# A second unit's inverses, masks and last weight piece moved in the written order of a fused attention and expert kernel

## The chip, the cores and the metric

The kernel runs on one core of a Trainium2 chip. Its engines work side by side and wait for each other on semaphores: TensorE (PE, with its weight loads shown apart as PEld), VectorE (DVE), ScalarE (ACT), GpSimd (POOL) and SyncE (SP), which here only issues transfers. ACT can issue transfers too. The metric is the time of one execution on the device in microseconds. Four runs of the kernel before gave a median of 562.54 us (561.25 to 563.91).

## The reference

The first half is a gated linear recurrence over 4 batches, 8 heads, 768 tokens and a head width of 48; the second is an expert layer with an ELU between two products, over 3072 tokens, 384 columns and 2048 hidden columns.

```python
f = 1.0 / (1.0 + np.exp(-f_logit))
for t in range(S):
    state = f[:, :, t, :, None] * state + np.einsum('bhd,bhe->bhde', k[:, :, t], v[:, :, t])
    y[:, :, t] = np.einsum('bhd,bhde->bhe', q[:, :, t], state)
...
h = x @ w_in
g = np.where(h > 0.0, h, alpha * (np.exp(np.minimum(h, 0.0)) - 1.0))
return (g @ w_out).astype(np.float32)
```

The attention inputs are float32. The two weight matrices arrive as float64, and the kernel makes float32 of them itself.

## The kernel before

The 3072 tokens are cut into 12 units of 256. A unit's attention is worked in closed form: `gates` makes 1 + exp(-f_logit) on ACT, `grow` (L630) its running product along the tokens on DVE, `fall` (L635) the inverse of that product, and `scale` (L625, POOL) multiplies k by the product and q by the inverse. Three pairs of heads lie in rows of their own and the fourth, pair `NKT`, is spread over the 16-row gaps beside them; `move` (L642) carries the product (`which` 0) or the inverse (`which` 1) of that fourth pair from the gaps into its own rows, in two transfers of 48 KB inside the on-chip memory. For unit 1 the inverse is moved on ACT's queue. Then `advance` (L736) makes the sums that update the states, `scores` (L713) the products of q and k, `mask` (L721) keeps the causal ones, `step` (L694, L699) adds up the states, and `outputs` (L751) and `carried` (L771) make the unit's tokens. `advance` and `outputs` write the same two PSUM banks, so `outputs` waits for the last `step` that reads them.

The weights come in 16 pieces n of 768 KB, one of `w_in` or `w_out` at a time, in the order in which unit 0 needs them. `fetch(n)` loads a piece into one of seven slots of `area`: a w_out piece in one transfer (L548), a w_in piece in a large one (L550, 576 KB) and two for the gaps (L553, 96 KB each). `split(n)` takes two DVE instructions (L567, L571), `lower(n)` one of ACT (L577), and `merge(n)` one of DVE (L585), which writes the float32 weights and then calls `fetch(n + 7)`. So each piece goes DVE, ACT, DVE.

Every transfer reports on one of eight semaphores, which are taken in turn by transfers of SP and ACT alike. A transfer that takes a semaphore again first waits, on the queue that issues it, for the landing of the transfer that had it before.

Everything is written out by hand and each engine runs its instructions in the written order. Work ahead of the loop does unit 0's attention and unit 1's gates. Then comes a loop over steps T (L1176). Two steps make one pair P = T // 2, which is 256 hidden columns of one unit; unit 0 has T = 0 to 15, unit 1 starts at T = 16. An even step does, in this order: `elu(P - 1)` on DVE (L955), whatever `plan` holds for the step, and `up` (for unit 0 L946: 12 matmuls, then Relu and Exp on ACT, L933 and L934). An odd step does the plan and then `down(P - 2)` (for unit 0 L978). At the end of each step the pieces in `later` are split and lowered. From unit 1 on, `up7` (L901) and the lower half of `down` (L1003) use seven products in the place of eight. Their PSUM tiles `psH` are two buffers in rotation, so the second half of `up7(8)` writes where pair 7 of unit 0 was, and waits for `elu(7)` to have read it.

What stands where around the change, before: pieces 2 to 15 are merged at the step of their number and split and lowered two steps earlier; pieces 10 and 11 are lowered at step 10. Unit 1's inverse is moved at step 3 (`F1`), its q of pair `NKT` scaled at step 5, and `both(1)` (advance, scores, masks, states) is planned for step 8 (`A1[1]`), which is before `up(4)`. Piece 15 is split and lowered at step 13, `gates(2)` is planned for step 14 and so lies ahead of `up(7)` and its Relu and Exp. `combine` starts at step 16, and so does unit 2's `grow`.

Of the kernel before, what the change touches and what calls it, by code (L numbers as in the profile page):

```python
# [356 lines left out]
def fast(ctx: ExitStack, tc: tile.TileContext, q, k, v, f_logit, w_in, w_out, out, flag, outer):  # L357
# [18 lines left out]
    nc = tc.nc  # L376
# [7 lines left out]
    NC = U // C  # L384
# [3 lines left out]
    NFT = DFF // 128  # L388
    NKT = DM // 128
# [4 lines left out]
    LAG = 2  # L394
    AHEAD = 7
    WA = 1
    F1 = 3
    W0 = 3
    SMALL = 16
    MORE = 5  # L400
# [2 lines left out]
    A1 = (2, 8, 10, 11)  # L403
# [207 lines left out]
    def gates(u, pieces=(NKT,), bias=1):  # L611

        p = 0
        for n in pieces:
            a = qkf[u % NB]["f"][:, p : p + n, 0]
            nc.scalar.activation(a, a, AF.Exp, scale=-1.0)
            if bias:
                nc.scalar.activation(a, a, AF.Copy, bias=1.0)
            p += n

    def scale(u, *todo):

        t = qkf[u % NB]
        for n, p, e in todo:
            e.tensor_tensor(out=t[n][:, p], in0=t[n][:, p], in1=t["f"][:, p, "kq".index(n)], op=ALU.mult)  # L625
# [6 lines left out]
    def fall(u, p):  # L632

        f = qkf[u % NB]["f"]
        nc.vector.reciprocal(f[:, p, 1], f[:, p, 0])  # L635

    def move(u, which, queue):

        f = qkf[u % NB]["f"]
        for r in range(2):  # L640
            to = PAD + D * r
            queue.dma_start(out=f[to : to + D, NKT, which], in_=f[GAP[r] : GAP[r] + PAD, 0:NKT, which])  # L642

    def decays(u, p):
        grow(u, p)
        fall(u, p)
        scale(u, ("k", p, nc.gpsimd))
        if p:
            scale(u, ("q", p - 1, nc.gpsimd))
        if p == NKT - 1:  # L650
            move(u, slice(0, 2), nc.sync if u > 1 else nc.scalar)

    def watch(u):
        nc.vector.scalar_tensor_tensor(
            out=fine[:], in0=qkf[u % NB]["f"][:, 0:NKT, 0, U - 1 :], scalar=LIMIT, in1=fine[:],
            op0=ALU.is_le, op1=ALU.mult,
        )

    def settle(u):

        watch(u)
        scale(u, ("q", NKT - 1, nc.gpsimd), ("k", NKT, nc.gpsimd), ("q", NKT, nc.gpsimd))
# [22 lines left out]
    def step(u, c):  # L685

        if u % UPB == UPB - 1 and c == NC - 1:
            return
        new = pus[u][c % 2][:, c // 2]
        box = boxes[(u * NC + c) % len(boxes)]  # L690
        s = box[:].rearrange("n (p d) -> n p d", d=64)[:, 0:HP, PAD:]
        if u % UPB or c:
            old = sts[u, c][:].rearrange("n (p d) -> n p d", d=64)[:, 0:HP, PAD:]
            nc.vector.tensor_tensor(out=s, in0=new, in1=old, op=ALU.add)  # L694
        else:
            nc.scalar.copy(s, new)
        if c == NC - 1:
            end = qkf[u % NB]["f"][:, :, 1, U - 1 :].broadcast_to([128, HP, D])
            nc.vector.tensor_tensor(out=s, in0=s, in1=end, op=ALU.mult)  # L699
        sts[(u, c + 1) if c < NC - 1 else (u + 1, 0)] = box  # L700

    def scores(u, banks=("a0", "a1"), pairs=range(HP), pc=None):

        t = qkf[u % NB]
        if pc is None:
            ats[u] = sb.tile([128, 2, NW, HP, C], FP32, tag="at", name=f"at{u}", bufs=1)
            pc = [ps.tile([128, NW, HP, C], FP32, tag=banks[r], name=f"psS{u}_{r}") for r in range(2)]
        for p in pairs:
            for w in range(NW):
                for b in range(2):  # L710
                    cols = slice(w * W + b * C, w * W + b * C + C)
                    for r in range(2):
                        nc.tensor.matmul(  # L713
                            pc[r][FULL[b], w, p], lhsT=t["k"][FULL[r], p, cols], rhs=t["q"][FULL[r], p, cols],
                            start=True, stop=True,
                        )
        return pc

    def mask(u, pc):
        for r in range(2):  # L720
            nc.vector.tensor_tensor(  # L721
                out=ats[u][:, r].rearrange("k w p i -> k (w p) i"), in0=pc[r][:].rearrange("k w p i -> k (w p) i"),
                in1=twice[:].unsqueeze(1).broadcast_to([128, NW * HP, C]), op=ALU.mult,
            )

    def advance(u, pairs=range(HP)):

        if u not in pus:
            pus[u] = [ps.tile([128, NW, HP, D], FP32, tag=n, name=f"psU{u}_{n}") for n in ("a0", "a1")]
        pu = pus[u]  # L730
        for p in pairs:
            for w in range(NW):
                for r in range(2):
                    h = 2 * p + r
                    for b in range(2):
                        nc.tensor.matmul(  # L736
                            pu[b][FULL[r], w, p], lhsT=kn[FULL[b], p, w, FULL[r]],
                            rhs=vs[u % NB][FULL[b], w, PAD + h * D : PAD + (h + 1) * D],
                            start=(w == 0 and p == 0), stop=(w == NW - 1 and p == HP - 1), skip_group_check=True,
                        )  # L740

    def outputs(u, banks=("a0", "a1")):


        pys[u] = [ps.tile([128, NW, HP, C], FP32, tag=banks[b], name=f"psY{u}_{b}") for b in range(2)]
        at = ats.pop(u)
        for w in range(NW):
            for p in range(HP):
                for r in range(2):
                    for b in range(2):  # L750
                        nc.tensor.matmul(  # L751
                            pys[u][b][FULL[r ^ b], w, p], lhsT=of_head(u, b, w, r, p),
                            rhs=at[FULL[b], r, w, p], start=(w == 0 and p == 0), stop=False,
                            skip_group_check=True,
                        )

        for b in range(2):
            nc.scalar.copy(between[:], pys[u][b][:, :, :, 0])
# [71 lines left out]
    plan, later = {}, {}  # L830

    def at_step(step, *todo):
        plan.setdefault(step, []).extend(todo)

    def both(u):

        advance(u)
        mask(u, scores(u, ("m3", "m0")))
        for c in range(NC):
            step(u, c)  # L840

    def attention(u, first, then):

        kept = []
        for p, i in enumerate(first):
            at_step(i, (lambda: settle(u)) if p == NKT else lambda p=p: decays(u, p))
        if u > 1:
            at_step(then[0], lambda: transposed(u, 0, "a0"), lambda: transposed(u, 1, "a1"))
        if len(then) == 4:
            at_step(then[1], lambda: both(u))  # L850
        else:
            at_step(then[1], lambda: advance(u))
            at_step(then[2], *(lambda c=c: step(u, c) for c in range(NC)))
            at_step(then[3], lambda: kept.append(scores(u)), lambda: mask(u, kept[0]))
        if u > 1:
            at_step(then[-2], lambda: outputs(u))
        at_step(then[-1], lambda: carried(u))
# [277 lines left out]
    scale(1, ("k", 0, nc.gpsimd), ("q", 0, nc.gpsimd), ("k", 1, nc.gpsimd), ("k", 2, nc.gpsimd))  # L1135
    scale(1, ("k", NKT, nc.gpsimd))
    fall(1, 2)
    watch(0)
    watch(1)
    scale(1, ("q", 1, nc.gpsimd), ("q", 2, nc.gpsimd))  # L1140
    at_step(A1[2], lambda: outputs(1), lambda: lower(A1[2]), lambda: lower(A1[2] + 1))
    for n in range(1, NFT):
        t = min(max(needs[n][0] - 2, 0), n)
        at_step(t, lambda n=n: merge(n))
        if n > 1:
            later.setdefault(max(t - 2, 0), []).append(n)
    at_step(F1, lambda: move(1, 1, nc.scalar))
    at_step(F1 + 2, lambda: scale(1, ("q", NKT, nc.gpsimd)))
    at_step(A1[0], lambda: transposed(1, 0, "a0"), lambda: transposed(1, 1, "a1"))
    at_step(4, lambda: warm(0, "m3", SMALL))  # L1150
    at_step(22, lambda: warm(0, "a0", MORE))
    attention(1, (), A1)
    at_step(8, lambda: load(2))
    at_step(14, lambda: gates(2))
    attention(2, D2, A2)
    weights = combine()
    for n in range(NFT):
# [5 lines left out]
    for u in range(3, NU):  # L1163
        t = (u - 1) * NFT
# [5 lines left out]
    for n in range(NR):  # L1170
        t = 3 * NFT + (NU - 4) * NFT * n // NR + RR
# [4 lines left out]
    for T in range(NU * NFT):  # L1176
        P = T // 2
        sevens = order[P][0] >= DIRECT
        if T % 2 and sevens:
            joined(P)  # L1180
        if T % 2 == 0 and P and order[P - 1][0] < DIRECT:
            elu(P - 1)
        for f in plan.pop(T, ()):
            f()
        if T % 2 == 0:
            up(P)
        elif P >= LAG and T not in joint:
            if T - 2 in joint:
                down(P - LAG - 1)
            down(P - LAG)  # L1190
        for n in later.pop(T, ()):
            split(n)
            if n not in (A1[2], A1[2] + 1):
                lower(n)
# [53 lines left out]
```

## Time and profile before

| | |
|---|---|
| median of four runs | 562.54 us (561.25 to 563.91) |
| profiled execution | 561.57 us |
| its span, first to last instruction | 559.7 us |
| mean granted TensorE clock | 0.996 |
| PE busy | 543.3 us (97%) |
| DVE busy | 407.0 us (73%) |
| ACT busy | 227.8 us (41%) |
| POOL busy | 292.3 us (52%) |

The page gives shares of the whole span, and the change works in its first 77 us alone. Views that show order are therefore of more use than sums: the chain of work that ended last, in order of time; the timeline of one engine in a window; and the waits, which name who released whom. Times inside the profile count from its first instruction. In a timeline each row has a start, a duration, the engine (SPq and ACTq for transfers that are issued), the line, the tiles written and read, the number of instructions merged into the row, and in brackets the idle time before it with what ended it. A merged row's duration reaches from its first start to its last end, waits included.

### The profile page before, as it was taken

To read this page: it belongs to the slowest core of one execution; us is meant where nothing else is said; L and a number is where in the kernel's file an instruction comes from. 1 tells how busy PE (TensorE), PEld (TensorE's weight loads), DVE (VectorE), ACT (ScalarE), POOL (GpSimd) and SP (SyncE) were. 2 spreads that over 40 slices of the span, in tenths; PEclk is the share of its full clock that TensorE was granted. 3 is DMA by queue.
4 is the path that set the end of the run, shared out by engine and by line. 5 is a ranking of instruction groups with operands and counts; after the bars stand their busy time and mean duration, and the time that the engine had idled before them with its cause. 6 is when DMAs were issued, how large, how long until landed. Compare 5 with 4: busy or idle time off the path is not lost.

```text
span 559.7 us, 15627 instructions
## 1 busy us (share of the span) xinstructions
PE 543.3 (97%) x6358; PEld 508.0 (91%) x6358; DVE 407.0 (73%) x804; ACT 227.8 (41%) x442; POOL 292.3 (52%) x567
## 2 busy tenths in 40 slices
PE   6899989999999999999999999999999999999996
PEld 3477768999999999999999999999999999999995
DVE  8988989786676786785785785786687777735553
ACT  3287853434343333434434343343333343333331
POOL 6600898475374375365466367357257348325332
PEclk9999989999999999999999999999999999999999
DMA  8998971024025226216207207207207302201101
GB/s 205 246 268 241 269 178 43 3 59 113 2 57 146 57 50 170 65 27 181 81 13 193 81 9 191 85 9 191 87 8 188 90 9 71 87 5 33 31 2 35
DMA packets 39474, 54.30 MB, mean 97 GB/s; under 512 B 4032, under 2 KB 29216, under 8 KB 39392
## 3 DMA queue, kind: packets, MB, share of 16 engines
q1 hardware_dynamic: 38592, 52.61, 36.0%
q8 instruction: 52, 0.85, 0.7%
q10 hardware_dynamic: 800, 0.59, 0.5%
q14 instruction: 30, 0.25, 0.2%
HBM read 45.02 MB, written 4.72 MB: 89 GB/s over the span
## 4 chain that ended last, share of the span: by engine, by line
PE 85%; DMA 7%; DVE 3%; ACT 3%; issue 1%; POOL 1%; ACTq 0%; SPq 0%; DVEq 0%; POOLq 0%
PE psH L901 39%; PE psM L1003 36%; DMA area<-in_moe_w_in_dram 4%; PE psY L771 2%; PE psY L751 2%; PE psU_a L736 2%; PE psS L713 2%; ACT area L577 2%; PE psT L673 1%; PE psM L978 1%; DMA f<-f 1%; DMA k<-in_k_dram 1%; DMA area<-in_moe_w_out_dram 1%; DVE bits L567 1%; DVE wi L585 1%
## 5 line engine op out<-in xcount | busy, mean ns | idle before, releaser
L901 PE MATMUL psH<-xt,wi 128*128 128x128 f32 (+1 forms) x1056 | 195.8, 295 | 0.0
L965 POOL TENSOR_TENSOR sums<-gg 128x128 f32<-128x128 f32 x176 | 77.4, 461 | 210.1 <-DVE gg L955 186.9
L933 ACT ACTIVATE gg<-hh 128x512 f32<-128x512 f32 x88 | 55.5, 630 | 252.0 <-DVE hh L923 111.3
L901 PEld LDWEIGHTS psH<-xt,wi 128*128 128x128 f32 x1056 | 150.0, 192 | 1.6
L901 PE MATMUL psH<-xt,area 128*128 128x128 f32 x704 | 121.9, 275 | 2.0 <-DVE gg L955 2.0
L901 PEld LDWEIGHTS psH<-xt,area 128*128 128x128 f32 x704 | 106.8, 192 | 6.8 <-DVE gg L955 2.2
L910 DVE TENSOR_TENSOR hh<-psH,u 128x256 f32<-128x256 f32 x88 | 37.0, 420 | 99.6 <-ACT u L908 99.6
L1003 PE MATMUL psM<-area,sums 128*128 128x192 f32 x528 | 102.1, 326 | 0.1
L1003 PEld LDWEIGHTS psM<-area,sums 128*128 128x128 f32 x528 | 88.0, 190 | 0.2 <-issue 0.2
L1003 PE MATMUL psM<-wo,gg 128*128 128x192 f32 x352 | 73.9, 332 | 0.0
L955 DVE SCALAR_TENSOR_TENSOR gg<-gg,hh 128x512 f32<-128x512 f32 x88 | 63.1, 717 | 1.5 <-ACT gg L934 1.5
L635 DVE RECIPROCAL f<-f 128x256 f32<-128x256 f32 x36 | 62.8, 1748 | 1.1
L934 ACT ACTIVATE gg<-gg 128x512 f32<-128x512 f32 x96 | 60.5, 631 | 3.0
L1003 PEld LDWEIGHTS psM<-wo,gg 128*128 128x128 f32 x352 | 56.3, 190 | 1.4
L923 DVE TENSOR_TENSOR hh<-psH,u43h 128x256 f32<-128x256 f32 (+1 forms) x176 | 54.7, 352 | 3.0
L965 POOL TENSOR_TENSOR sums<-gg,sums 128x128 f32<-128x128 f32 x88 | 46.7, 531 | 6.9
L625 POOL TENSOR_TENSOR q<-q,f 128x256 f32<-128x256 f32 x48 | 39.7, 828 | 18.5 <-DMA area<-in_moe_w_in_dram 14.7
L923 DVE TENSOR_TENSOR u43h<-psH,hh 128x256 f32<-128x256 f32 x88 | 37.1, 421 | 9.4 <-PE psH L901 9.0
L625 POOL TENSOR_TENSOR k<-k,f 128x256 f32<-128x256 f32 x48 | 39.2, 819 | 7.8 <-DMA f<-f 5.5
L965 POOL TENSOR_TENSOR sums<-sums,gg 128x128 f32<-128x128 f32 x88 | 43.3, 492 | 0.0
L1003 PE MATMUL psM<-area,gg 128*128 128x192 f32 x176 | 43.0, 326 | 0.0
L1003 PE MATMUL psM<-wo,sums 128*128 128x192 f32 x176 | 43.0, 326 | 0.0
(100 smaller groups left out, 649.2 us busy)
## 6 DMA issues: line engine op xcount, KB each, us to landing
area<-in_moe_w_out_dram SPq DMA_DIRECT2D x8, 768.0 KB, 10.4
again<-in_moe_w_in_dram SPq DMA_DIRECT2D x16, 384.0 KB, 4.3
again<-in_moe_w_out_dram SPq DMA_DIRECT2D x16, 384.0 KB, 3.6
k<-in_k_dram SPq DMA_DIRECT2D x12, 384.0 KB, 4.5
q<-in_q_dram SPq DMA_DIRECT2D x12, 384.0 KB, 5.6
v<-in_v_dram SPq DMA_DIRECT2D x12, 384.0 KB, 6.1
area<-in_moe_w_in_dram SPq DMA_DIRECT2D x8, 576.0 KB, 8.9
out_dram<-o SPq DMA_DIRECT2D x42, 96.0 KB, 2.6
```

Source lines behind the costliest of these rows:

```text
L577: nc.scalar.activation(raw.bitcast(U16)[:, 2::4], raw.bitcast(U32)[:, 0::2], AF.Copy, scale=2.0**-29)
L625: e.tensor_tensor(out=t[n][:, p], in0=t[n][:, p], in1=t["f"][:, p, "kq".index(n)], op=ALU.mult)
L635: nc.vector.reciprocal(f[:, p, 1], f[:, p, 0])
L713: nc.tensor.matmul(pc[r][FULL[b], w, p], lhsT=t["k"][FULL[r], p, cols], rhs=t["q"][FULL[r], p, cols], start=True, stop=True,)
L901: nc.tensor.matmul(to, lhsT=lhs, rhs=rhs, start=(n == 0), stop=True, skip_group_check=True)
L910: add = lambda to, x, y: nc.vector.tensor_tensor(out=to, in0=x, in1=y, op=ALU.add)
L923: add = lambda to, x, y: nc.vector.tensor_tensor(out=to, in0=x, in1=y, op=ALU.add)
L933: nc.scalar.activation(g[:], h, AF.Relu, scale=-1.0)
L934: nc.scalar.activation(g[:], g[:], AF.Exp, scale=-1.0)
L955: nc.vector.scalar_tensor_tensor(out=g[:], in0=g[:], scalar=-1.0, in1=phs.pop(P), op0=ALU.add, op1=ALU.max)
L965: nc.gpsimd.tensor_tensor(out=s[:, i], in0=x, in1=y, op=op)
L1003: nc.tensor.matmul(pm[bank][:, half * DH : (half + 1) * DH], lhsT=x, rhs=y, start=first, stop=(j == NP - 1), skip_group_check=True,)
```

## The change

Five things move in the written order; no instruction is added or taken away on any engine.

- `move(1, 1, nc.scalar)` goes from step 3 to just behind unit 1's last reciprocal, `fall(1, 2)`, ahead of the loop. It stays on ACT's queue.
- The scaling of unit 1's q of pair `NKT` on POOL, which needs that move, goes from step 5 to ahead of the loop.
- `both(1)` is cut in two: advance, scores and masks go to the end of step 7, ahead of the split of piece 9, and the four states stay at step 8.
- Piece 15 is split and lowered at the end of step 14 in the place of step 13, so behind `up(7)` and its Relu and Exp.
- `gates(2)` goes from step 14 to step 15, behind the lowering of piece 15.

In the built program the two moved transfers also take two other semaphores, two turns of the eight earlier than before, and the transfers of SP between the old and the new place shift by two.

```diff
-    def both(u):
-
-        advance(u)
-        mask(u, scores(u, ("m3", "m0")))
-        for c in range(NC):
+    def both(u, part=3):
+
+        if part & 1:
+            advance(u)
+            mask(u, scores(u, ("m3", "m0")))
+        for c in range(NC if part & 2 else 0):
             step(u, c)
...
-            at_step(then[1], lambda: both(u))
+            at_step(then[1], lambda: both(u, 3 if u > 1 else 2))
...
     fall(1, 2)
+    move(1, 1, nc.scalar)
     watch(0)
     watch(1)
-    scale(1, ("q", 1, nc.gpsimd), ("q", 2, nc.gpsimd))
+    scale(1, ("q", 1, nc.gpsimd), ("q", 2, nc.gpsimd), ("q", NKT, nc.gpsimd))
...
         if n > 1:
-            later.setdefault(max(t - 2, 0), []).append(n)
-    at_step(F1, lambda: move(1, 1, nc.scalar))
-    at_step(F1 + 2, lambda: scale(1, ("q", NKT, nc.gpsimd)))
+            later.setdefault(max(t - (1 if n == NFT - 1 else 2), 0), []).append(n)
...
-    at_step(14, lambda: gates(2))
+    at_step(15, lambda: gates(2))
...
             down(P - LAG)
+        if T == A1[1] - 1:
+            both(1, 1)
         for n in later.pop(T, ()):
             split(n)
```

More of the change, by code (lines that the diff above doesn't have):

```diff
@@ L396, in fast @@
     WA = 1
-    F1 = 3
     W0 = 3
```

## The prediction

> **What bounds the kernel now.** I read the page first, for which engine is full and when; then the chain of work that ended last, in order of time; then PE's timeline and waits; last SP's and DVE's timelines at the places that the change touches.
>
> From the page: PE is busy nearly everywhere but in the first slices, and DVE is full there.
>
> ```profile
> PE 543.3 (97%) x6358; PEld 508.0 (91%) x6358; DVE 407.0 (73%) x804; ACT 227.8 (41%) x442; POOL 292.3 (52%) x567
> PE   6899989999999999999999999999999999999996
> DVE  8988989786676786785785785786687777735553
> ```
>
> Over 77 to 552 us the table by windows gives PE 474.81 busy of 475.00. So from 77 us on PE is the bound without a gap, and the change can move the end only by moving the moment at which that begins. The chain in order of time shows what sets it:
>
> ```profile
> 69.56 1.57 ACT area L577
> 71.24 2.01 ACT area L577
> 73.25 0.65 ACT f L616
> 73.91 0.84 ACT f L618
> 74.76 0.49 ACT gg L933
> 75.28 0.64 ACT gg L934
> 75.94 0.70 DVE gg L955
> 76.68 2.80 PE psH L901 x12
> ```
>
> ACT lowers pieces 14 and 15, does `gates(2)`, then Relu and Exp of pair 7; DVE does `elu(7)`; then PE may go on. PE's timeline shows what it lost (idle time in brackets):
>
> ```profile
> 55.17 0.29 PE L751 MATMUL psY<-at,v 64*64 64x64 f32 x2 [0.50 <-DVE state L694]
> 55.63 1.16 PE L751 MATMUL psY<-at,v 64*64 64x64 f32 x62 [0.17 <-DVE state L694]
> 71.04 2.74 PE L978 MATMUL psM<-wo,gg 128*128 128x384 f32 x8
> 76.68 0.71 PE L901 MATMUL psH<-xt,area 128*128 128x128 f32 x4 [2.01 <-DVE gg L955]
> ```
>
> From 36 us on that is 0.35 + 0.19 before two `up`s (DVE merges), 0.67 at `outputs(1)` and 2.01 at `elu(7)`. A wait before the last one saves nothing unless `elu(7)` comes earlier too: the 2.01 would only grow.
>
> **The end of the prologue (piece 15 and gates(2)).** DVE's timeline of before:
>
> ```profile
> 68.59 0.99 DVE L585 CUSTOM_DVE_ANT_0 wo<-area,bits 128x1536 uint16<-128x1536 uint16 x1 [0.68 <-ACT area L577]
> 70.97 0.68 DVE L955 SCALAR_TENSOR_TENSOR gg<-gg,psH 128x512 f32<-128x512 f32 x1
> 71.57 1.00 DVE L585 CUSTOM_DVE_ANT_0 wo<-area,bits 128x1536 uint16<-128x1536 uint16 x1
> 73.28 0.97 DVE L585 CUSTOM_DVE_ANT_0 wo<-area,bits 128x1536 uint16<-128x1536 uint16 x1 [0.70 <-ACT area L577]
> 75.94 0.69 DVE L955 SCALAR_TENSOR_TENSOR gg<-gg,psH 128x512 f32<-128x512 f32 x1 [1.70 <-ACT gg L934]
> ```
>
> These are merge 13, `elu(6)`, merge 14, merge 15 and `elu(7)`; split 15 stood at 69.62 to 71.05, beside ACT's work. After the change ACT is free for Relu and Exp of pair 7 as soon as lower 14 ends at 71.5 (PE's `up(7)` ends at 71.2), so they end at about 72.6 and not 75.9. But merge 15 (step 15) still stands ahead of `elu(7)` (step 16) on DVE, and split 15 has come behind merge 14, which waits for lower 14. The new chain from lower 14's start at 69.56: lower 14 1.95; merge 14 1.0; split 15, two instructions, 1.2 (two of 0.56 with gaps, as at 50.01) to 1.45 (two of 0.70, as at 69.62 beside POOL's work); lower 15 1.95; merge 15 0.92 to the next start; `elu(7)` 0.69; some 0.04 at each of four hand-overs. Sum 7.9 to 8.1, and `elu(7)` ends at 77.4 to 77.7 where it ended at 76.63: **+0.8 to +1.05, I take +0.9**. In short, between lower 14's end at 71.51 and `elu(7)` stood 4.4 us of ACT (the rest of lower 15, gates, Relu, Exp); now merge 14, split 15, lower 15 and merge 15 stand there, 5.1 to 5.3 on two engines in turn, and gates, Relu and Exp are beside them.
>
> `gates(2)` now starts behind lower 15, at about 75.7, and takes 1.7 (72.97 to 74.67), so it ends at 77.4; `grow` of unit 2, next on DVE, starts behind `elu(7)` at 77.5. It costs nothing, with a margin of 0.1; without that cover it would only delay DVE, which has PE's next need (`hh`, 79.91 for PE at 82.58) ready 2 us early. ACT's copy for `up7(8)`, queued behind the gates, goes from 75.81 to 77.4, ahead of the same `hh`.
>
> **Masks ahead of split 9.** Before, DVE sat idle from 48.91 to 50.01 for piece 9's landing, then ran split 9, `elu(3)`, merge 8, masks (52.55, 1.20 to the next start) and states without a pause until the fourth state ended at 55.48. Scores ended on PE at 49.31. If the masks fill that idle time they start at 49.4, split 9 at 50.6, and all from there is 0.6 earlier: `outputs(1)`, then lowers 10 to 14, which ran back to back with DVE up to lower 12 and on ACT from there. That passes whole to lower 14's start: **-0.6** at best. What is queued behind the masks' wait for scores is split 9 and with it lower 9; both have slack, as merge 9 came at 56.87.
>
> **The inverse moved early.** On ACT the two issues (0.57 and 0.62) leave 38.44, where ACT was executing lower 4 anyway, and go to 30.45, behind the reciprocal that ends at 30.40. Relu of pair 0, queued behind them, started at 31.63 and starts at 31.7; its Exp is followed by 0.30 of idle time, so nothing. POOL's scaling (1.11 us at 45.92) then waits for the landing and nothing stands behind it until 58.30; q is needed at 48.2. It also leaves bits of piece 8, which took 0.97 beside it against 0.56 elsewhere.
>
> The transfers are where it costs. Before, SP's issue of piece 9 took the semaphore of the moved inverse and waited for its landing:
>
> ```profile
> SPq L548 <- DMA f<-f: 5.5, 1, 5.5
> 27.33 0.32 SPq L550 DMA_DIRECT2D area<-in_moe_w_in_dram  x1
> 30.78 3.26 SPq L553 DMA_DIRECT2D area<-in_moe_w_in_dram  x2
> 45.44 0.39 SPq L548 DMA_DIRECT2D area<-in_moe_w_out_dram  x1
> f<-f ACTq DMA_DIRECT2D x2, 48.0 KB, 6.8
> ```
>
> (the waits of SP's queue, three rows of its timeline, and the transfers issued at 38.4 to 42.4). That wait is gone. In the built program its place is taken by piece 6's two gap transfers, the row at 30.78, each of which now waits for one of the moves; pieces 7, 8 and 9 are behind them on SP. So it turns on when a move that is issued at 30.45 lands. In the row above it took 6.8 us, at about the time the weights issued before it landed (piece 8's part issued at 34.76, 10.8 to landing, so 45.6); in 38.4 to 42.4 us the queue table shows 450 packets of SP's queue and none of ACT's. Ahead of 30.45 stands piece 6's large part, issued at 27.33 with 12.0 to landing. So the moves land at about 39.2 (38.7 to 39.6), and the weight stream runs dry.
>
> The restart: gaps issued at 39.25 and 39.85, pieces 7 and 8 at 40.45 and 41.05. A 768 KB transfer in a nearly empty queue took 4.5 (45.44), a small move at best 2.7, and a piece in a full stream about 2.9 (piece 7 landed at 43.3, the gap before it at 40.4). So the gaps land at 42.2, piece 7 at 45.1, 8 at 47.9, 9 at 50.8; before it was 40.4, 43.3, 46.1, 49.9. On DVE: split 6 at 42.3 (was 41.76), split 7 at 45.2 (43.82), split 8 at 48.0 (46.47), masks at 49.95 (split to masks 1.93), split 9 at 51.15, fourth state 4.27 later at 55.4 (55.48). PE is not held meanwhile: `down(1)` at 44.54 needs merge 5, which ends at about 44.4. So the late stream eats what the masks gain: **0.0**, bounds -0.6 (stream in time) and +1.0 (every landing 1 us later). Pieces 10 to 15 then come about when they did, since the dry stretch of before (44 to 46.5) is gone.
>
> [...]
>
> **Sum.** 0.9 + 0.0 = +0.9. Profiled execution: span 559.7 to 560.6, time 561.57 to 562.5. That profile lies 1.0 under the median of the runs, so against the median I forecast 563.4, which is 0.16% up. About 0.3% (1.7 us) is what a measurement of this kernel can tell from no change.
>
> **The rivals.**
>
> - *The moves land early* and the stream stays full: then -0.6 + 0.9 = +0.3, 562.8. For it: they are small. Against: the five pairs on record took 3.9 to 7.1 us in a busy stream. Chance 0.12.
> - *A later restart* ends slower. At SP's queue from 39.2 on, pieces 7 to 9 come 1 us or more after my times, bits of piece 8 start past 49.0, masks past 50.9, and the states end past 56.4; with the 0.9 that is over 1.7. Price at 1 to 2 us late: 564.4 to 565.4. For it: pieces took up to 4.3 us (10, 49.9 to 54.2). Against: the last restart was quick. Chance 0.22.
> - *The end is freed*: `elu(7)` comes right behind Exp of pair 7, the whole 2.01 and perhaps the 0.6 go: 560 to 560.5. For it: ACT has 3.7 less in front. Against: merge 15 stands before it on DVE in the written order. Chance 0.06.
> - The forecast itself: 0.60.
>
> **How the numbers follow.** Forecast and early landing lie within 0.3% of before (560.85 to 564.23): 0.72, less some for the spread of the runs, 0.69. The late restart gives slower, 0.24; the freed end and an unknown gain, 0.07. The range starts below the early landing by the runs' spread, 562.0, and reaches into the late restart, 565.2.
>
> **What would show it.** ACT's Exp of pair 7 before lower 15, and DVE idle before merge 15 by about 1.8 us on ACT; PE idle of 2 to 3.5 us before `up7(8)`'s second half, released by `elu(7)`; SP's L553 rows of piece 6 at about 39 and a DMA share that falls at 40 us and not at 45; splits 6 to 8 waiting for transfers; the masks right at 50. Wrong would be: L553 issued at 33 to 34, or `elu(7)` ending before 76.6.

## The result and the profile after

The changed kernel takes 563.83 us (median of 43 runs, 561.47 to 565.96) beside 562.71 us of the kernel before on the same chip (69 runs, 560.37 to 564.32). The ratio is 1.0022, with a 95% interval from 1.0014 to 1.0029: 1.24 us slower (0.8 to 1.6), which lies within the 0.3% that the chances were given for. The profiled execution took 562.25 us, with a span of 560.5 (before: 561.57 and 559.7). Both lie under the medians, by 1.6 and 1.1 us, so their rows are examples and not averages. The ratio is not worked out from the two medians and can differ from their quotient, by up to 0.1% in the runs below. Executions far slower than all others are left out of it, which concerns two of the last kernel, e12 (798 and 1430 us, cause not known).

The rows of 40 slices on the page of after show no more than those of before: PE full nearly everywhere, and a tenth more or less at the front.

```profile
PE   6789979999999999999999999999999999999996
DVE  8898979786676786785795785786687777735553
```

The timelines say more. DVE's, of after (start, duration, engine, line, operation, tiles, shapes, count, and in brackets the idle time with what ended it):

```profile
44.66 0.56 DVE L566 TENSOR_SCALAR bits<-area 128x768 int32<-128x768 int32 x1 [0.43 <-DMA area<-in_moe_w_out_dram]
...
48.45 0.56 DVE L566 TENSOR_SCALAR bits<-area 128x768 int32<-128x768 int32 x1 [1.17 <-DMA area<-in_moe_w_in_dram]
...
50.39 1.28 DVE L720 TENSOR_TENSOR at<-psS,twice 128x512 f32<-128x512 f32 x2
51.59 0.55 DVE L566 TENSOR_SCALAR bits<-area 128x768 int32<-128x768 int32 x1
...
72.04 0.96 DVE L584 CUSTOM_DVE_ANT_0 wo<-area,bits 128x1536 uint16<-128x1536 uint16 x1 [1.13 <-ACT area L576]
72.92 0.82 DVE L566 TENSOR_SCALAR bits<-area 128x768 int32<-128x768 int32 x1
73.77 0.70 DVE L570 TENSOR_SCALAR area<-area 128x768 int32<-128x768 int32 x1
76.46 0.96 DVE L584 CUSTOM_DVE_ANT_0 wo<-area,bits 128x1536 uint16<-128x1536 uint16 x1 [1.99 <-ACT area L576]
77.33 0.68 DVE L955 SCALAR_TENSOR_TENSOR gg<-gg,psH 128x512 f32<-128x512 f32 x1
77.97 0.72 DVE L629 TENSOR_TENSOR_SCAN f<-f 128x256 f32<-128x256 f32 x1
...
80.81 0.41 DVE L910 TENSOR_TENSOR hh<-psH,u 128x256 f32<-128x256 f32 x1
...
107.55 1.22 DVE L720 TENSOR_TENSOR at<-psS,twice 128x512 f32<-128x512 f32 x2
```

Splits 7 and 8 now wait for weights; the masks of unit 1 stand between split 8 and split 9. Below, merge 14, split 15, merge 15, `elu(7)` and the scan of unit 2 (`grow`) follow each other, with waits of 1.13 and 1.99 us for lowers 14 and 15 on ACT. ACT's own timeline, of after, has the two moves at the front and Relu and Exp of pair 7 before lower 15 and `gates(2)`:

```profile
30.92 1.22 ACTq L641 DMA_DIRECT2D f<-f  x2
...
71.75 0.68 ACT L933 ACTIVATE gg<-psH 128x512 f32<-128x512 f32 x1
72.46 0.63 ACT L934 ACTIVATE gg<-gg 128x512 f32<-128x512 f32 x1
74.51 1.92 ACT L576 ACTIVATE area<-area 128x768 uint16<-128x768 uint32 x1 [1.41 <-DVE area L570]
76.17 0.89 ACT L615 ACTIVATE f<-f 128x768 f32<-128x768 f32 x1
77.10 0.84 ACT L617 ACTIVATE f<-f 128x768 f32<-128x768 f32 x1
...
97.45 0.63 ACT L933 ACTIVATE gg<-hh 128x512 f32<-128x512 f32 x1 [2.36 <-DVE hh L923]
...
101.29 0.25 ACT L908 COPY u<-psH 128x128 f32<-128x128 f32 x1
```

The last two rows are used further down.

PE's timeline of after: the wait at `elu(7)` has grown from 2.01 to 3.03 us, and there is one more at unit 2's scores, with outputs of unit 2 that are stretched (1.44 us against 1.16).

```profile
55.54 0.29 PE L750 MATMUL psY<-at,v 64*64 64x64 f32 x2 [0.42 <-DVE state L693]
56.00 1.16 PE L750 MATMUL psY<-at,v 64*64 64x64 f32 x62 [0.17 <-DVE state L693]
...
78.07 0.71 PE L901 MATMUL psH<-xt,area 128*128 128x128 f32 x4 [3.03 <-DVE gg L955]
...
104.81 1.16 PE L712 MATMUL psS<-q,k 64*64 64x64 f32 x64 [0.35 <-PE psM L1003]
...
108.54 1.44 PE L750 MATMUL psY<-at,v 64*64 64x64 f32 x64
```

In before, PE's timeline has scores and outputs of unit 2 without a wait, and DVE's has unit 2's masks just ahead of the outputs:

```profile
104.29 1.16 PE L713 MATMUL psS<-q,k 64*64 64x64 f32 x64
108.02 1.16 PE L751 MATMUL psY<-at,v 64*64 64x64 f32 x64
106.69 1.22 DVE L721 TENSOR_TENSOR at<-psS,twice 128x512 f32<-128x512 f32 x2
```

The view puts the wait of 0.35 us down to PE's own work before it. By the kernel's code it is DVE's states: unit 2's scores write the two PSUM banks that its states read, and the last of these states ends at 104.70. The outputs need the masks, the second of which ends at 108.77 in after.

In the waits of SP's queue (line, what it waited for: us in total, times, longest) the gap transfers of piece 6 wait for the moves:

```profile
SPq L552 <- DMA f<-f: 8.0, 1, 8.0
```

They were issued at 38.13 and 38.74, right behind the moves' landing at 38.11 and 38.60. The view of the transfers in 38 to 44 us (40 equal slices, the busy share of the DMA engines in tenths) shows the weight stream all but empty for the first 1.5 us:

```profile
DMA  1000000200656525769466479999999998999899
```

One view is left aside. The chain of work of after, from 69 to 83 us, puts `elu(7)` behind a load of `f` that it ends at 77.35. DVE's row for `elu(7)` has no idle time before it: merge 15 was still there. The chain names the last semaphore of several, and here it is the wrong one.

**One offset to keep in mind.** In the execution shown of after, everything from `up(0)` on is 0.43 us later than in that of before (29.19 against 28.76), ahead of all that the change touches. So `elu(7)`, which ends 1.39 us later (78.02 against 76.63), is 0.96 later by the change.

### The profile page after: what moved, and what is told of

Its sections match the earlier page's. It is cut to its first block, busy times and chain, and to the rows that moved or that the text cites. A ratio compares the mean times of both kernels' runs of the same rounds, so it can differ in the third digit from the quotient of the medians.

```text
span 560.5 us, 15626 instructions
## 1 busy us (share of the span) xinstructions
PE 542.1 (97%) x6358; PEld 507.2 (90%) x6358; DVE 406.2 (72%) x804; ACT 227.9 (41%) x442; POOL 292.9 (52%) x567
## 4 chain that ended last, share of the span: by engine, by line
PE 89%; DMA 5%; DVE 3%; POOL 1%; issue 1%; ACT 0%; SPq 0%; ACTq 0%; DVEq 0%; POOLq 0%
PE psH L901 39%; PE psM L1003 36%; DMA area<-in_moe_w_in_dram 4%; PE psY L750 2%; PE psY L770 2%; PE psU_a L735 2%; PE psM L978 2%; PE psS L712 2%; PE psH L946 1%; PE psT L672 1%; PE psW L1060 1%; DMA f<-f 1%; DMA f<-in_f_logit_dram 1%; DVE area L570 0%; DVE bits L566 0%
## 5 line engine op out<-in xcount | busy, mean ns | idle before, releaser
L901 PE MATMUL psH<-xt,wi 128*128 128x128 f32 (+1 forms) x1056 | 195.0, 294 | 0.0
L901 PEld LDWEIGHTS psH<-xt,wi 128*128 128x128 f32 x1056 | 149.5, 192 | 1.6
L901 PE MATMUL psH<-xt,area 128*128 128x128 f32 x704 | 121.8, 275 | 3.0 <-DVE gg L955 3.0
L901 PEld LDWEIGHTS psH<-xt,area 128*128 128x128 f32 x704 | 106.5, 191 | 7.9 <-DVE gg L955 3.2
```

What stands on the lines that cost most here:

```text
L901: nc.tensor.matmul(to, lhsT=lhs, rhs=rhs, start=(n == 0), stop=True, skip_group_check=True)
```

## The experiments

Changes in us are against the kernel before, measured on the same chip, with the 95% interval of the ratio in us behind them.

| kernel | what it has | change in us |
|---|---|---|
| after | all five moves | +1.24 (0.8 to 1.6) |
| e1 | move, scaling and masks early | +0.1 (-0.8 to +1.0) |
| e2 | piece 15 and `gates(2)` late | +1.7 (0.8 to 2.5) |
| e3 | after, merge 15 behind `elu(7)` | +1.3 (0.3 to 2.3) |
| e4 | `gates(2)` late | -1.0 (-1.7 to -0.3) |
| e5 | piece 15 late | +1.4 (0.6 to 2.25) |
| e6 | masks early | -0.2 (-1.0 to +0.7) |
| e7 | move and scaling early | -0.1 (-1.1 to +1.0) |
| e8 | masks early, `gates(2)` late, first `combine` ahead of the scan | -1.5 (-2.25 to -0.6) |
| e9 | before, first `combine` issued five times | +2.9 (2.0 to 3.7) |
| e10 | `gates(2)` late, first `combine` ahead of the scan | -0.8 (-1.9 to +0.2) |
| e11 | after, `gates(3)` six steps earlier | +1.2 (0.4 to 2.1) |
| e12 | e8, `gates(3)` six steps earlier | -1.9 (-2.9 to -0.9) |

**The two halves.** e1 is before with the early half of the change:

```diff
     fall(1, 2)
+    move(1, 1, nc.scalar)
...
-    at_step(F1, lambda: move(1, 1, nc.scalar))
-    at_step(F1 + 2, lambda: scale(1, ("q", NKT, nc.gpsimd)))
...
+        if T == A1[1] - 1:
+            both(1, 1)
```

> The kernel before with the first half of the change alone: unit 1's inverse moved behind its last reciprocal, its q scaled ahead of the loop, and the masks ahead of split 9; piece 15 and the third unit's gates stay where they were. My theory (the weight stream runs dry behind the moves and eats what the masks gain): states of unit 1 end within 0.3 us of before, time 0.0 us (-0.3 to +0.4), and SP issues piece 6's gap transfers at 38 to 40 us. Rival, that the early move is free: -0.6 us. Rival, that the first half carries the loss of the changed kernel: +0.8 us or more.

Measured: 562.85 us against 562.75, ratio 1.0002 (0.9986 to 1.0018). SP's queue waited for the moves here too, in its waits of e1:

```profile
SPq L553 <- DMA f<-f: 10.5, 1, 10.5
```

e2 is before with the late half:

```diff
-            later.setdefault(max(t - 2, 0), []).append(n)
+            later.setdefault(max(t - (1 if n == NFT - 1 else 2), 0), []).append(n)
...
-    at_step(14, lambda: gates(2))
+    at_step(15, lambda: gates(2))
```

> The kernel before with the second half alone: piece 15 split and lowered at step 14, gates(2) at step 15. My theory: elu(7) ends at about 77.5 us where it ended at 76.6, behind merge 15, and the time rises by 0.9 us (0.5 to 1.3), which is all that the whole change costs. Rival, that the loss is in the first half: 0.0.

Measured: 564.12 us, ratio 1.003 (1.0015 to 1.0044). So the front half comes to +0.1 us, with 0.9 us open either way, and the loss is found in the end half, as forecast.

**The end half, one part at a time.** e5 has only the `later` line of e2, e4 only its `gates` line.

> The kernel before with piece 15 alone split and lowered one step later; gates(2) stays at step 14, ahead of up(7). My theory: this is what costs. Merge 15 ends 1.0 us later and elu(7) and the scan of unit 2 stand behind it on VectorE, so +1.0 us (0.6 to 1.7), as much as the whole second half. Rival, that the second half's loss comes from the gates behind piece 15: 0.0 here.

Measured: 563.89 us against 562.64, ratio 1.0025 (1.0011 to 1.004). DVE's timeline of e5 has merge 15 and `elu(7)` behind lower 15, as the working had it. Counted from `up(0)`, which starts at 30.25 here, `elu(7)` is 1.36 us later than in before, where 1.0 was expected:

```profile
77.89 0.98 DVE L585 CUSTOM_DVE_ANT_0 wo<-area,bits 128x1536 uint16<-128x1536 uint16 x1 [2.06 <-ACT area L577]
78.79 0.68 DVE L955 SCALAR_TENSOR_TENSOR gg<-gg,psH 128x512 f32<-128x512 f32 x1
```

> The kernel before with gates(2) alone moved to step 15; piece 15 stays at step 13. Relu and Exp of pair 7 then follow lower 15 at once and elu(7) starts at about 74.3 in the place of 75.9. Theory A (TensorE's wait at elu(7) sets the end): -1.6 us. Theory B (VectorE's work from the scan of unit 2 on sets it): the scan waits for the gates until about 76.0 in the place of 76.5, so -0.6 us (-0.3 to -0.9). If gates(2) was rightly the part that costs: +0.5 or more.

Measured: 561.71 us against 562.75, ratio 0.9982 (0.997 to 0.9995). With the gates out of their way, Relu and Exp of pair 7 follow lower 15 directly, and `elu(7)` comes as soon as merge 15 is done. That was at 75.64 and not at the expected 74.3, since lower 14 starts at 70.84 in this execution and at 69.56 in that of before. But then the scan waits for the gates. DVE's timeline of e4:

```profile
75.64 0.69 DVE L955 SCALAR_TENSOR_TENSOR gg<-gg,psH 128x512 f32<-128x512 f32 x1
77.24 0.90 DVE L630 TENSOR_TENSOR_SCAN f<-f 128x256 f32<-128x256 f32 x1 [0.92 <-ACT f L618]
```

and PE's timeline of e4, where the 2.01 us at `elu(7)` have come down to 0.20 and other waits, all for `hh` of DVE or ahead of unit 2's scores, have come up:

```profile
76.38 0.71 PE L901 MATMUL psH<-xt,area 128*128 128x128 f32 x4 [0.20 <-DVE gg L955]
80.97 0.49 PE L901 MATMUL psH<-xt,wi 128*128 128x128 f32 x2 [0.20 <-DVE hh L910]
88.13 0.68 PE L901 MATMUL psH<-xt,area 128*128 128x128 f32 x4 [0.63 <-DVE hh L923]
```

PE was freed of 1.8 us and the time fell by 1.0. Alone the two parts measure -1.0 and +1.4, together +1.7; the intervals leave open whether that is more than the sum of the two. With piece 15 late, the gates' new place still brings `elu(7)` forward by 0.6 us against `up(0)` (e2 against e5), but no gain shows in the time.

**Is it the wait at `elu(7)`?** e3 takes that wait out of the changed kernel: merge 15 goes one step on, behind `elu(7)`.

```diff
-        at_step(t, lambda n=n: merge(n))
+        at_step(t + (n == NFT - 1), lambda n=n: merge(n))
```

> The changed kernel with merge 15 one step later, so behind elu(7) on VectorE. Then elu(7) needs only split 15 in front of it and ends at about 75, and TensorE's idle time of 3.0 us ahead of the second half of up7(8) all but goes. Theory A, as I forecast it (that wait sets the end): 2.5 to 3 us less than the changed kernel, 1.3 to 1.8 us less than before. Theory B, from the trace of the changed kernel (VectorE, busy without a pause from there to 98 us, and gates(2) ahead of its scan set the end; TensorE waits for it later, at scores and outputs of unit 2): scan still starts at about 77.5 to 78, so the time stays as the changed kernel's, 1.0 to 1.4 us over before, with TensorE idle at scores(2) and outputs(2) instead.

Measured: 563.53 us against 562.75, ratio 1.0023 (1.0005 to 1.0041): as slow as after. DVE's timeline of e3 shows `elu(7)` early, and merge 15 and the gates now ahead of the scan (the scan's wait is put down to a load, but `gates(2)` ended on ACT at 80.05):

```profile
76.50 0.67 DVE L955 SCALAR_TENSOR_TENSOR gg<-gg,psH 128x512 f32<-128x512 f32 x1
78.58 1.04 DVE L584 CUSTOM_DVE_ANT_0 wo<-area,bits 128x1536 uint16<-128x1536 uint16 x1 [1.40 <-ACT area L576]
80.09 0.80 DVE L629 TENSOR_TENSOR_SCAN f<-f 128x256 f32<-128x256 f32 x1 [0.47 <-DMA f<-in_f_logit_dram]
...
83.52 0.41 DVE L910 TENSOR_TENSOR hh<-psH,u 128x256 f32<-128x256 f32 x1
```

PE's timeline of e3 has no wait at `elu(7)` any more, 0.79 us at POOL's `blend` a little earlier, and 1.98 us at the first `hh`:

```profile
76.94 0.49 PE L901 MATMUL psH<-xt,area 128*128 128x128 f32 x2 [0.79 <-POOL xt L889]
...
83.98 0.49 PE L901 MATMUL psH<-xt,wi 128*128 128x128 f32 x2 [1.98 <-DVE hh L910]
```

PE's wait only moved. Theory B had expected the scan at 77.5 to 78, and it came at 80.09: of B the time came true, not this row. The profiled execution, 565.14 us, is also the second slowest of twelve with a median of 563.53. Its rows show where the wait went, not what a typical execution loses.

What is common to these executions is a run of work beside PE that begins at unit 2's scan. In after it goes over DVE from 77.97 to the `hh` that ends at 97.4, with one pause of 0.25; then over ACT from 97.45 to 101.54 without a pause (Relu, Exp, four key copies, `gates(3)`, the copy of `u`: the last two rows of ACT's fence above); then over DVE again, from 101.57 to unit 2's states (end 104.70, and PE's scores start at 104.81) and masks (107.55).

**Is it DVE's run?** e9 adds DVE work there to the kernel before and nothing else:

```diff
-                nc.vector.tensor_tensor(
-                    out=to[:, n : n + 2], in0=x[:, n : n + 2], in1=y[:, n : n + 2], op=ALU.subtract
-                )
+                for _ in range(5 if n == 0 and to is t[0] else 1):
+                    nc.vector.tensor_tensor(
+                        out=to[:, n : n + 2], in0=x[:, n : n + 2], in1=y[:, n : n + 2], op=ALU.subtract
+                    )
```

> The kernel before, with the first combine instruction on DVE (between unit 2's first reciprocal and the first hh, at 78.99 us of the profile before) issued five times, to the same result: four more instructions of 0.41 to 0.55 us, 1.7 to 2.2 us of DVE work, and nothing else changed. Theory P (the forecast's: from 77 us on PE is the bound and DVE has hh ready about 2 us before PE needs it): the added work fits into the margin and the time stays, 0 to +0.3 us. Theory D (DVE sets the pace from unit 2's scan to unit 2's masks and states, with some 0.1 us to spare at the outputs of unit 2): hh, masks and the end all come later by about the work added, +1.2 to +2.1 us; the outputs of unit 2 start at about 109.7 in place of 108.0, with waits of PE before them that DVE releases.

Measured: 565.07 us against 562.41, ratio 1.0051 (1.0035 to 1.0066), 2.9 us. The added work turned out larger than expected. DVE's timeline of e9:

```profile
79.94 3.91 DVE L870 TENSOR_TENSOR area<-wo 128x384 f32<-128x384 f32 x5
83.77 0.41 DVE L911 TENSOR_TENSOR hh<-psH,u 128x256 f32<-128x256 f32 x1
```

Five took 3.91 us where the one of before took 1.00, so 2.91 us were added, and the time rose by 2.9 (2.0 to 3.7). P, with 0 to 0.3, falls, and with the larger work too: its margin in before was 2.26 us (from 80.32, where `hh`'s first instruction ends, to 82.58), which would leave a loss of 0.65. D's size was off because 0.41 to 0.55 us was assumed for an instruction of which one followed every 0.73 us here. PE's timeline of e9 has the wait where DVE's work was put:

```profile
84.23 0.49 PE L902 MATMUL psH<-xt,wi 128*128 128x128 f32 x2 [2.26 <-DVE hh L911]
```

D had also expected PE to wait at unit 2's outputs, and it did not: this is its only wait behind `elu(7)` up to there, and from 86.05 on its rows are drawn out: four L902 matmuls took 1.49 us that had taken 0.82 at 78.13, and the eight of L979 3.36 for 2.75. Ahead of the wait they are as short as after's at a granted clock of 1.00 (2.75 us for the eight in both). So e9 shows that with such rows the margin at the first `hh` is at most 0.65 us (2.91 added, 2.26 waited), and not 2. The wait alone lies within the measured 2.0 to 3.7. That the run over DVE and ACT goes on to set the pace up to unit 2's masks is not shown by e9; it rests on the rows of after above, and on those of e1 and e7 below.

All profiled executions in one table, with the start of `elu(7)`, the start of the first `hh`, the span, and what is left of the span behind each:

| kernel | `elu(7)` | `hh` | span | span - `elu(7)` | span - `hh` |
|---|---|---|---|---|---|
| before | 75.94 | 79.91 | 559.7 | 483.8 | 479.8 |
| after | 77.33 | 80.81 | 560.5 | 483.2 | 479.7 |
| e1 | 76.97 | 80.56 | 560.0 | 483.0 | 479.4 |
| e2 | 78.19 | 81.67 | 561.2 | 483.0 | 479.5 |
| e3 | 76.50 | 83.52 | 563.3 | 486.8 | 479.8 |
| e4 | 75.64 | 80.50 | 560.6 | 485.0 | 480.1 |
| e5 | 78.79 | 82.76 | 562.7 | 483.9 | 479.9 |
| e6 | 77.65 | 81.13 | 561.6 | 484.0 | 480.5 |
| e7 | 77.68 | 81.30 | 561.4 | 483.7 | 480.1 |
| e8 | 75.64 | 79.78 | 560.1 | 484.5 | 480.3 |
| e9 | 76.84 | 83.77 | 563.4 | 486.6 | 479.6 |
| e10 | 74.70 | 78.74 | 558.9 | 484.2 | 480.2 |
| e11 | 77.22 | 80.70 | 560.8 | 483.6 | 480.1 |
| e12 | 74.37 | 78.62 | 557.9 | 483.5 | 479.3 |

The span follows DVE's first `hh` within 1.2 us over all of them, and `elu(7)` only within 3.8. It is e3 and e9, which put work between the two, that make the difference: without them the 3.8 are 2.0.

**The front half, one part at a time.** e7 is before with the early move and scaling alone (e1's diff without the masks), e6 with the masks alone.

> The kernel before with the inverse's move and its scaling alone ahead of the loop; masks stay at step 8. My theory: SP's gap transfers of piece 6 wait for the moves, piece 8 lands about 2 us late, and the states of unit 1 end 0.3 us later: +0.3 us (0.0 to 0.7), which is what the masks' gain pays for in the first half. Rival, that the early move is free: 0.0, with split 9 no longer waiting for piece 9.

Measured: 563.00 us against 562.64, ratio 0.9999 (0.9981 to 1.0017). Of the moves that were issued from 32.74 on the first landed 6.8 us later, SP's L553 waited 9.0 us for them and was issued at 39.59, and splits 8 and 9 waited 0.78 and 0.23 us for weights. The run can't tell the expected +0.3 from nothing.

> The kernel before with the masks alone ahead of split 9; the inverse is moved at step 3 as before. My theory: the masks fill VectorE's idle time ahead of piece 9, the states of unit 1 end 0.6 us earlier against the end of scores, and the time falls by 0.6 us (0.3 to 0.9), since nothing holds back the weight stream here. Rival, that the masks' place gives nothing: 0.0.

Measured: 563.04 us against 562.64, ratio 0.9997 (0.9982 to 1.0013). DVE's timeline of e6:

```profile
49.98 1.29 DVE L721 TENSOR_TENSOR at<-psS,twice 128x512 f32<-128x512 f32 x2 [0.44 <-PE psS L713]
...
59.29 0.78 DVE L567 TENSOR_SCALAR bits<-area 128x768 int32<-128x768 int32 x1 [1.52 <-DMA area<-in_moe_w_out_dram]
```

The masks went into DVE's idle time, and the fourth state ended 26.13 us behind `up(0)` where it was 26.72: the 0.6 that the working had. But split 11 then waited 1.52 us for piece 11, which landed at 59.2. In the profile of before split 11 waits for nothing; in those of e2 and e4, without early masks, it waits 0.67 and 0.28. So in this execution the weight stream took the masks' gain back, with no early move to blame. How much of the 0.6 is left on average the run can't tell.

**A version that beats both.** If DVE's run decides, the first `combine` instruction (L869), which stands between the reciprocal and `hh`, is better placed in the wait for the gates that e4 shows. e8 is before with the masks early, the gates late and this:

```diff
-    attention(2, D2, A2)
     weights = combine()
-    for n in range(NFT):
+    at_step(CB, lambda: next(weights))
+    attention(2, D2, A2)
+    for n in range(1, NFT):
         at_step(CB + n, lambda: next(weights))
```

> The kernel before with the masks ahead of split 9 and gates(2) at step 15, and one thing more: the first of combine's instructions ahead of unit 2's scan on VectorE, which waits 0.9 us for the gates in the run with gates(2) late alone. Piece 15 and the moved inverse stay as before. Theory B (VectorE's work from elu(7) to the masks of unit 2 sets the end): 0.6 from the masks and 0.6 to 1.5 from elu(7) and combine in idle time, so -1.2 to -2.1 us, and hh of pair 8 starts about 2 us earlier against the end of scores of unit 1. If only TensorE's wait counted: -2.2 us, and combine's place would not matter.

Measured: 561.34 us against 562.64, ratio 0.9974 (0.996 to 0.9989). DVE's timeline of e8:

```profile
76.25 0.55 DVE L870 TENSOR_TENSOR area<-wo 128x384 f32<-128x384 f32 x1
77.25 0.83 DVE L630 TENSOR_TENSOR_SCAN f<-f 128x256 f32<-128x256 f32 x1 [0.45 <-ACT f L618]
...
79.78 0.36 DVE L911 TENSOR_TENSOR hh<-psH,u 128x256 f32<-128x256 f32 x1
```

`elu(7)` is at 75.64 as in e4, the wait for the gates has shrunk from 0.92 to 0.45, and `hh` comes 2.53 us behind the scan's start instead of 3.26. e10 is e8 without the masks:

> The kernel before, with gates(2) at step 15 and the first combine instruction ahead of unit 2's scan; masks, move and piece 15 as before. It is the kernel e8 without the masks' move. Theory D without a gain of the masks (as the run with the masks alone had it): the first hh comes at 79.8 to 80.0 with up(0) at 28.8, as in e8, and the time is that of e8, -1.1 to -1.7 us. If the masks' move gave a part of e8's gain, this is 0.4 to 0.6 us slower than e8: -0.7 to -1.1. Theory P, by which PE's start behind elu(7) alone counts (0.3 us earlier with gates late): the same as gates late alone, -1.0 us, or less.

Measured: 561.53 us against 562.41, ratio 0.9986 (0.9967 to 1.0004). That is between e4 and e8 and can't be told from either, so the masks' share of e8 stays open.

**Is the run beside PE the only bound?** In e11 and e12 `gates(3)` leaves ACT's part of it, for a place (step 18) where ACT is idle:

```diff
-        at_step(t - 8, lambda u=u: gates(u))
+        at_step(t - (14 if u == 3 else 8), lambda u=u: gates(u))
```

> The changed kernel with the gates of unit 3 six steps earlier, at step 18 in the place of 24, where ACT has 4.3 us of idle time and the copy of u behind them has 2 us to spare before hh. Theory D in full (the run that sets the pace goes from unit 2's scan on DVE to its hh at 96.8, over ACT's Relu, Exp, key copies, gates(3) and copy of u to 101.5, and over DVE again to the states and masks of unit 2): the 1.7 us of gates(3) leave that run, DVE's wait of 2.73 us for u falls to about 1.1, the wait of 0.35 at unit 2's scores and the stretched outputs (1.44 for 1.16) go, and the time is some 0.6 us below the changed kernel, so +0.3 to +0.9 over before. If PE alone decides, PE's rows stay where they are and the time is that of the changed kernel, +1.2.

Measured: 563.53 us against 562.25, ratio 1.0022 (1.0008 to 1.0037), the same as after; the gain of 0.6 is within the interval, but nothing shows it. In PE's timeline of e11 the waits at the scores and in the outputs are gone:

```profile
77.96 0.71 PE L901 MATMUL psH<-xt,area 128*128 128x128 f32 x4 [2.79 <-DVE gg L955]
...
105.59 1.16 PE L712 MATMUL psS<-q,k 64*64 64x64 f32 x64
...
109.31 1.16 PE L750 MATMUL psY<-at,v 64*64 64x64 f32 x64
```

And still the scores start 0.78 later than in after. In this execution PE's rows are drawn out from 79.17 on (the eight L978 matmuls of 79.86 took 4.18 us, those of 86.31 took 2.75), and its rows show no wait from 77.96 to the outputs: here PE is the bound, and what starts it is `elu(7)`. DVE now waits for it, 1.81 us for `u` where 1.1 was expected, 0.32 of that ACT's wait for PE.

> The kernel of e8 (masks early, gates(2) late, first combine ahead of the scan) with the gates of unit 3 at step 18 as in e11. Theory D: the 0.26 at unit 2's scores and the 0.28 in its outputs go, 0.5 us less than e8, so -1.7 to -2.3 against before. If gates(3) are not on the run that sets the pace: the time of e8, -1.5.

Measured: 560.86 us against 562.25, ratio 0.9966 (0.9948 to 0.9984). In the profiled execution the mean granted clock was 0.999, and PE started behind `elu(7)` at 75.11 and had no wait at the scores (102.87) and the outputs (106.60); on the way it still waited 0.52 and 0.34 us for `hh`. The interval holds both what D had and the time of e8, so the gain over e8 is not shown, and e8 is the version to take from here.

So two runs stand side by side in this stretch, close together: PE's from `elu(7)`, and the one from unit 2's scan over DVE and ACT; after's waits at the scores and in the outputs, 0.63 us in sum, are what the second had over the first. Work added to the second passes into the time (e9), work taken from it alone showed no gain (e11, where 0.6 us can't be excluded), and an earlier start of PE does not pay where the second run starts later (e3).

## Why the prediction was right, and where its reason was not

The forecast was 563.4, +0.9, "within 0.3%" as the likeliest; measured were +1.24 (0.8 to 1.6) and 563.83. Point by point:

- **End of the prologue, +0.9.** The order of events is as worked out: Exp of pair 7 before lower 15, merge 15 and then `elu(7)`. From lower 14's start to the end of `elu(7)` it took 7.93 us (forecast 7.9 to 8.1), and against `up(0)`, `elu(7)` came 0.96 later (forecast 0.8 to 1.05). Split 15's first instruction took 0.82 us, above the 0.56 and 0.70 of its bounds. e2 gives +1.7 (0.8 to 2.5) in time, which holds the term at its edge.
- **`gates(2)` at no cost, with a margin of 0.1.** In after the gates end at 77.94 and the scan starts at 77.97, with `elu(7)` before it until 78.02: a tie. By the prediction's own terms the margin was nil rather than 0.1, since 1.7 us of gates stand beside merge 15's 0.92, `elu(7)`'s 0.69 and two hand-overs of 0.04. What was not seen is that late gates alone gain 1.0 us (e4), and that with piece 15 in its new place no such gain shows.
- **Early moves.** Issued at 30.92 and 31.52, landed 7.2 and 7.1 us later; forecast 39.2 for the landing, measured 38.1 and 38.6. The gaps landed at 41.4 and 41.8 (forecast 42.2), piece 7 at 44.6 (45.1), piece 8 at 48.4 (47.9), piece 9 at 50.7 (50.8). The stream ran dry, splits 7 and 8 waited, and the rival that the moves land early is out.
- **Masks ahead of split 9.** They started at 50.39 (49.95 forecast, 0.43 of it the offset named above). Relative to `up(0)` the fourth state ended 0.06 us earlier than before; the working had 0.08. Front half 0.0, and e1 measured +0.1 (-0.8 to +1.0). e6 adds that the 0.6 would not have stayed whole without the move either.
- **The step that failed** is the first one: "So from 77 us on PE is the bound without a gap, and the change can move the end only by moving the moment at which that begins." e3 took PE's wait at `elu(7)` away and gained nothing; e9 added 2.9 us of DVE work behind it and lost 2.9. For the same reason the change does not work in the first 77 us alone, as was said ahead of the prediction, but up to unit 2's outputs at 108 us. The same error stands in the gates' part, by which a delay of DVE would cost nothing because `hh` is "ready 2 us early". That margin is the one at the first hand-over alone. The run over DVE and ACT has hardly a pause after it, and in before it came to unit 2's outputs with little to spare: its masks start at 106.69 and PE's outputs at 108.02. In after the masks start 0.86 later, PE's scores wait 0.35 us, the outputs start 0.52 later and are stretched by 0.28. These two make 0.80 us, the change of the span; but 0.43 of it is the offset that the change did not make, so this one pair of executions shows 0.37 where the medians show 1.24. The first `hh` came only 0.47 later against `up(0)`, because the `combine` instruction ahead of it took 0.49 us in after and 1.00 in before. The number came out because `elu(7)` and the scan stand next to each other on DVE, so that the wait for lower 15 delayed both runs by nearly the same (0.96 and 1.00 against `up(0)`). That was luck: the working looked at one of the two. The rival "the end is freed" rested on the same step: e3 all but met its condition, and the 560 to 560.5 did not come.

What hid this in the profile of before is the clock. The table by windows, of before (window, us and PE busy, count, granted clock, DMA share, GB/s):

```profile
77.00:100.00 23.00, 23.00 (x148) 0.93 0.35 80
```

and of after:

```profile
77.00:100.00 23.00, 21.93 (x147) 1.00 0.35 82
```

Before, PE was busy all the time, but ran at half clock from 77.3 to 80.7 (0.50 granted in 77.30 to 80.70). That is 1.7 us of work lost, which a busy share doesn't show. What before would do there at a clock of 1.00 no execution shows. The nearest are e1 and e7, whose end half is that of before, though their clock at this place is not known: from the start of `elu(7)` to unit 2's scores they took 27.50 and 27.96 us, before 28.35 and after 27.48; PE waits 0.26 and 0.37 us at these scores, and the outputs take 1.44 us in both, as in after. After, PE starts 1.4 us later than before at this place, runs at a granted clock of 1.00, and has caught up by 82.30 (before 82.58). It gives that back in rows that are drawn out and in the 0.35 at the scores.

From issue to landing the moves took 7.1 us in after, 5.9 in e1 and, the first of the two, 6.8 in e7. The row of before that the forecast was built on had 6.8, the quickest move of that profile 2.7; of the two the row was the better guide here.

What stays open: the size of the end part, with +1.2 in after and +1.7 in e2; the share of the early masks in e8; why e3 has the time of after, though its scan started 1.0 us later against `up(0)` in the executions profiled; and how often PE's run and how often the other one decides, since of the two executions compared one had half clock in this stretch (before) and the other none (after).

## What to carry to other kernels

A busy share of 100% says that an engine had work, not that it had none to spare: look at its granted clock in the same window before calling it the bound (here 0.93 from 77 to 100 us, with 23.00 of 23.00 us busy). A margin at one hand-over is worth little if the engine that feeds it has no pause afterwards: follow that engine's timeline to the next place where it rests, and add work there to see if the time follows. And when instructions move on two engines at once, ask of each whether it stands ahead of the run that sets the pace: the gates did (-1.0 alone), and piece 15's merge in its new place did too (+1.4).

## What the runs showed of the hardware that was not expected

- In the profile of before PE's granted clock is 0.50 for 3.4 us, from 77.3 to 80.7, and 1.00 just ahead of that. It begins 0.6 us after an idle time of 2.01 us had ended, and the four L901 matmuls of 77.23 took 1.40 us. After's 3.03 us of idle time at nearly the same place were followed by a granted clock of 1.00 (77 to 90 us) and 0.82 us for these four, and the 3.02 us of e2 by the same 0.82. Behind the 2.38 us of e5 and the 2.79 of e6 they took 1.35 and 1.49 us, and behind the 2.79 of e11 0.82, with 4.18 for the eight of L978 that follow. The length of the idle time alone does not tell these apart, and what does is not shown.
- The mean granted clock of the profiled execution is 0.993 to 0.997 in eleven of the fourteen kernels, 0.998 in after and e10 and 0.999 in e12. In e3, e4 and e8 (0.995, 0.995 and 0.997) it is 1.00 in each of the ten windows from 77 to 552 us, so what they lost lies outside.
- The same DVE instruction of 128x384 elements (L869) took 0.49 us in after and 1.00 in before at the same place in the order, and in e9 five of them took 3.91. In before a POOL instruction from 78.85 to 79.57 covers its start at 78.99; in after POOL's ends at 80.45, just behind its start at 80.40. That this is the cause was not tested. The distance from the scan to the first `hh` so varies between 2.84 and 3.43 us in kernels that have the same instructions between them.
